# Batch 0's softmax of A by row exps on ScalarE, and a new order of work, in a fused attention and feed-forward kernel

## The chip, the cores and the metric

The kernel runs on one core of a Trainium2 chip. The metric is the device time of one execution in microseconds (us); the profile is one execution taken by the hardware profiler. Engines are PE (TensorE matmul), PEld (its weight loads), ACT (ScalarE), DVE (VectorE), POOL (GpSimd) and SP (SyncE). Each engine works through its own list of instructions in order and waits on semaphores for the others. DMA queues are fed by POOL (all loads) and SP (all stores but the last).

## The reference

Eight batches and eight heads of 576 tokens and 64 columns go through an attention with 32 landmarks (mean of 18 tokens each), and its output, as 4608 rows of 512, through a feed-forward layer of width 2048 with a squared relu. Inputs and output are f32.

```python
q_lm = q.reshape(B, H, m, S // m, D).mean(axis=3)        # m = 32, S = 576, D = 64
k_lm = k.reshape(B, H, m, S // m, D).mean(axis=3)
def sm(a, b):
    s = scale * np.matmul(a, b.transpose(0, 1, 3, 2))
    s = s - np.max(s, axis=-1, keepdims=True)
    e = np.exp(s)
    return e / (np.sum(e, axis=-1, keepdims=True) + 1e-09)
A, Bm, C = sm(q, k_lm), sm(q_lm, k_lm), sm(q_lm, k)
Z = Bm.transpose(0, 1, 3, 2) / (norm1(Bm) * norminf(Bm) + 1e-06)
for _ in range(6):
    Z = 2 * Z - Z @ Bm @ Z
x = (A @ Z @ C @ v).transpose(0, 2, 1, 3).reshape(4608, 512)
h = np.maximum(x @ w_in, 0.0)
out = (h * h) @ w_out
```

## The kernel before

The kernel never forms x. Per batch it makes Z·C·V, multiplies that by w_in (four chunks, W, whose copies to bf16, We, are the weights WP) and then multiplies A's transpose (AT) by it: F, the first feed-forward layer. R is the relu of an F (PSUM to the buffers RS, of which there are three), Q its square (RS to G), and O the second layer, by tiles of 128 tokens in four quarters of four matmuls each, with Oe as copy out of PSUM and St as store.

An operation has a name such as F0.16: kind, batch, number. Those that the text uses are, beside F, R, Q, O, W, We: SC and SA, the score matmuls for C and A; Amx, Asb, Aex, Asu, Arc, Aml, the maximum, subtraction, exp, sum, reciprocal and product of A's softmax (L959 to L971); Ap and Ab, A's transposition on PE and its copy to AT; Cmx, Cex and CT, C's maximum, exp with a running sum, and transposition; CV, C·V and CVe, its copy; N and U, matmuls and update of one Newton step; Yi and Zi, its start; Zd and Zm, the last Z spread and scaled; ZC and ZCe, Z·C·V and its copy; Bsb, Bex and so on, the same softmax for Bm; Btr, Bnm, Bad, Brn, Blo, its transposition and norms; bk, the product BK from which SA of batches 0 and 1 is made; lm, lmc, lme, landmarks, with LS as buffer; c0 to c18, constants; ldq, ldk (buffers X), ldv (V), lx (XS), win and wout, loads.

Batches 0 and 1 have A with tokens on the partitions: 18 row groups of 32 columns for each of the two head halves, 36 in all, in two parts (u = 0: 16 groups, u = 1: 20). In batch 0 each part is cut in two pieces a and b, so Asb0.1a and Aex0.1a work on 10 groups (128x320), Asb0.0a and Aex0.0a on 8 (128x256). For batch 0 the F's come in two parts of tokens too: F0.0 to F0.14 with 256 tokens, F0.16 to F0.30 with 320, a pair of ff-blocks each; the same for batch 1.

A text table, ORDER, lists every operation of the kernel in one sequence, with the PSUM banks after @ and, where there is a choice, the engine after a slash (A: ACT, D: DVE, P: POOL). A class Plan walks through it with a cost for each operation and puts dummy matmuls (a block of ones, L1177) into PE's gaps up to the first O0, which keep the granted clock up; the instructions are then emitted by the starts that this plan gives. So the table alone sets what stands where on each engine, and the plan's constants set only how the engines' lists are interleaved and where dummies go.

The lines of batch 0's A that the change touches, before:

```python
op(f"Amx{b}.{u}{z}", {"DVE": v_(w)}, ... nc.vector.tensor_reduce(s3(0)[:, at], p3_(pS)[:, at], axis=AX.X, op=ALU.max), ...)
op(f"Asb{b}.{u}{z}", {"DVE": v_(w)}, ... nc.vector.tensor_tensor(sa3[:, at], p3_(pS)[:, at], b3(0)[:, at], ALU.subtract), ...)
op(f"Aex{b}.{u}{z}", {"ACT": a_(w)}, ... nc.scalar.activation(sa3[:, at], sa3[:, at], AF.Exp), ...)
```

Of the kernel before, what the change touches and what calls it, by code (L numbers as in the profile page):

```python
# [7 lines left out]
P = 128  # L8
# [7 lines left out]
B = 8  # L16
# [18 lines left out]
N_RS = 3  # L35
# [19 lines left out]
class Plan:  # L55
# [44 lines left out]
    def schedule(self, order):  # L100
# [5 lines left out]
        for word in order:  # L106
# [5 lines left out]
            t = max([free[e], *(d.end + self.LAT[d.kind][i] for d in o.deps)])  # L112
# [17 lines left out]
            if e == "PE":  # L130
                free[e] += self.SWITCH * (o.mode != mode)
# [72 lines left out]
RATE = {"sw": 0.375e6, "hw": 0.2e6, "first": 0.385e6, "then": 0.4e6, "late": 0.3e6}  # L204
# [5 lines left out]
def a_(n):  # L210
    return 0.1 + 0.00084 * n
# [48 lines left out]
def pe(n, k=1):  # L260
    return k * max(n * 0.0004215, 0.027)
# [3 lines left out]
def kernel(  # L265
# [31 lines left out]
    LS = [mk(f"LS{i}", [P, 2, 256], F32) for i in range(2)]  # L297
# [55 lines left out]
    op("c3", {"DVE": 0.3}, lambda e: nc.vector.tensor_copy(ident[:], identf[:]),  # L353
# [991 lines left out]
```

## Time and profile before

| | |
|---|---|
| median of 3 runs | 263.11 us (262.78 to 264.88) |
| profiled execution | 263.91 us, its span 261.9 us |
| mean granted clock of PE | 0.999 |
| PE busy | 250.5 us, 96% of the span |
| DVE busy | 212.9 us, 81% |
| ACT busy | 176.3 us, 67% |
| POOL busy | 72.3 us, 28% |
| first F starts | 28.96 us |
| batch 1's first F starts | 53.74 us |
| last matmul ends | about 257.7 us |
| size of one load: X, w_in, w_out | 288, 256, 512 KB |

How to read the rows. In a timeline a row begins with start and duration in us; the brackets at its end give the idle time of the engine ahead of it and what released it. In a list of groups a row has line, engine, operation, names and shapes (partitions x elements), count, then busy us and mean ns of one, then idle time ahead and its releasers. A window row gives the window, its length, and the busy time of each engine with the count of instructions. Names in rows are those of buffers: ST is the Newton state, SA the scores of A, smA their maxima and sums, ps a PSUM bank, RS and G the relu's and the square's output, ZM the scaled Z, C the exps of C. Line numbers are those of the kernel before unless a row is from the kernel after.

### The profile page before, as it was taken

How to read it: one execution, taken by the hardware profiler on the slowest of the kernel's cores; microseconds unless marked ns; L12 is line 12 of the kernel's file. 1: busy time of each engine (PE TensorE's matmuls, PEld its weight loads, DVE VectorE, ACT ScalarE, POOL GpSimd, SP SyncE). 2: the span in 40 equal slices, each digit the busy share in tenths (PEclk: the TensorE clock that was granted, in tenths of full speed). 3: DMA queues.
4: the chain of work that ended last, by engine and by line, in shares of the span. 5: the costliest groups of instructions: out<-in, count | busy, mean ns of one | idle time of the engine just before them, and what ended most of it. 6: DMA issues, size and time to landing. Idle time of an engine off the chain costs nothing.

```text
span 261.9 us, 7574 instructions
## 1 busy us (share of the span) xinstructions
PE 250.5 (96%) x3098; PEld 140.4 (54%) x3098; DVE 212.9 (81%) x552; ACT 176.3 (67%) x325; POOL 72.3 (28%) x121
## 2 busy tenths in 40 slices
PE   7978998999999999999999999999999999999993
PEld 2565565566454556465554555565444556466542
DVE  3989799987899998978999899988999979746220
ACT  2533795859696889887765699796584674676412
POOL 8558878543500622352030210012100111000000
PEclk9999999999999999999999999999999999999999
DMA  6999999999997699999928193030302030051025
GB/s 99 206 198 201 208 206 207 207 212 224 241 218 156 100 213 222 231 169 237 208 38 165 17 201 90 0 83 1 83 17 68 21 83 20 3 121 40 3 68 132
DMA packets 25122, 34.17 MB, mean 130 GB/s; under 512 B 2432, under 2 KB 14464, under 8 KB 25088
## 3 DMA queue, kind: packets, MB, share of 16 engines
q0 software_dynamic: 19168, 24.25, 54.4%
q1 hardware_dynamic: 5760, 9.31, 13.9%
q8 instruction: 24, 0.39, 0.6%
q10 hardware_dynamic: 160, 0.13, 0.2%
q14 instruction: 10, 0.08, 0.1%
HBM read 48.50 MB, written 9.44 MB: 221 GB/s over the span
## 4 chain that ended last, share of the span: by engine, by line
PE 65%; DVE 20%; ACT 3%; issue 3%; POOL 1%; DVEq 0%; ACTq 0%; POOLq 0%
PE ps L1103 37%; PE ps L1056 17%; PE ps L892 3%; DVE G L1086 2%; ACT RS L1077 2%; DVE SA L1016 1%; DVE TT L470 1%; PE ps L735 1%; DVE smA L1020 1%; DVE sm L773 1%; DVE SA L1009 1%; PE ps L1177 1%; PE ps L821 1%; DVE RS L1079 1%; DVE smA L1012 1%
## 5 line engine op out<-in xcount | busy, mean ns | idle before, releaser
L1103 PE MATMUL ps<-w_out,G 128*128 128x512 bf16 (+1 forms) x592 | 139.4, 374 | 0.2 <-DVE LM L418 0.2
L1103 PEld LDWEIGHTS <-G 128*128 128x128 bf16 x592 | 54.4, 98 | 53.7 <-issue 6.2
L1077 ACT ACTIVATE RS<-ps 128x576 bf16<-128x576 f32 (+2 forms) x101 | 63.8, 656 | 23.8 <-PE ps L1056 15.4
L1056 PE MATMUL ps<-AT,WP 128*128 128x288 bf16 (+2 forms) x512 | 75.0, 286 | 1.1 <-DVE LM L531 1.1
L1056 PEld LDWEIGHTS <-WP 128*128 128x128 bf16 x512 | 48.0, 98 | 22.7 <-issue 2.5
L1084 ACT ACTIVATE G<-RS 128x576 bf16<-128x576 bf16 (+2 forms) x60 | 40.2, 685 | 1.8 <-DVE RS L1079 1.0
L1086 DVE TENSOR_TENSOR G<-RS 128x576 bf16<-128x576 bf16 (+2 forms) x63 | 29.3, 473 | 5.8 <-ACT RS L1077 5.3
L412 ACT COPY OS<-ps 128x512 f32<-128x512 f32 (+1 forms) x29 | 16.6, 571 | 19.0 <-PE ps L1103 15.2
L1079 DVE TENSOR_SCALAR RS<-ps 128x576 bf16<-128x576 f32 (+1 forms) x27 | 19.8, 735 | 10.0 <-PE ps L1056 8.8
L412 ACT CAST WP<-ps 128x1024 bf16<-128x1024 f32 (+1 forms) x24 | 22.4, 964 | 5.3 <-PE ps L892 5.2
L470 DVE STREAM_TRANSPOSE TT<-X 128x576 uint32<-128x576 uint32 x32 | 24.3, 762 | 0.4 <-DMA X<-in_q_dram 0.3
L636 POOL TENSOR_TENSOR BD<-ST,blkb 128x256 bf16<-128x256 bf16 x13 | 9.9, 758 | 49.3 <-DVE ST L713 42.2
L441 POOL DMA_DIRECT2D V<-in_v_dram x24 | 12.9, 539 | 25.2 <-PE ps L821 19.3
L776 ACT ACTIVATE C<-ps,sm 128x576 bf16<-128x576 f32 x16 | 14.2, 904 | 7.1 <-DVE sm L773 7.0
L713 DVE SCALAR_TENSOR_TENSOR ST<-ST,ps 128x128 bf16<-128x128 bf16 (+1 forms) x48 | 12.8, 267 | 6.0 <-PE ps L699 3.2
L1177 PE MATMUL ps<-onesb 128*128 128x512 bf16 (+1 forms) x43 | 12.4, 392 | 1.5 <-DVE onesb L348 1.5
L416 DVE CAST WP<-ps 128x1024 bf16<-128x1024 f32 (+1 forms) x10 | 11.6, 1161 | 1.6 <-PE ps L892 1.6
L773 DVE TENSOR_REDUCE sm<-ps 128x1 f32<-128x576 f32 x16 | 11.7, 744 | 0.2 <-PE ps L735 0.2
L1018 ACT ACTIVATE SA<-SA 128x640 f32<-128x640 f32 (+1 forms) x12 | 8.1, 685 | 4.8 <-DVE SA L1016 4.8
L892 PE MATMUL ps<-w_in,ZC 64*32 64x512 bf16 x256 | 10.7, 382 | 0.5 <-DVE ST L713 0.4
L657 POOL TENSOR_TENSOR ST<-Bf,sm 128x64 bf16<-128x64 f32 x5 | 1.5, 296 | 34.8 <-DVE sm L630 34.8
L1009 DVE STREAM_TRANSPOSE SA<-ps 128x320 f32<-128x320 f32 (+1 forms) x24 | 10.0, 453 | 0.9 <-PE ps L730 0.8
(140 smaller groups left out, 297.2 us busy)
## 6 DMA issues: line engine op xcount, KB each, us to landing
out_dram<-OS SPq DMA_DIRECT2D x70, 128.0 KB, 2.4
X<-in_k_dram POOLq DMA_DIRECT2D x16, 288.0 KB, 9.9
X<-in_q_dram POOLq DMA_DIRECT2D x16, 288.0 KB, 9.2
XS<-in_q_dram POOLq DMA_DIRECT2D x5, 576.0 KB, 11.6
XS<-in_k_dram POOLq DMA_DIRECT2D x5, 576.0 KB, 8.1
V<-in_v_dram POOLq DMA_DIRECT2D x8, 288.0 KB, 9.6
w_in<-in_moe_w_in_dram POOLq DMA_DIRECT2D x8, 256.0 KB, 9.4
w_out<-in_moe_w_out_dram POOLq DMA_DIRECT2D x4, 512.0 KB, 10.9
```

The source lines that it names most:

```text
L412: nc.scalar.copy(o, i)
L470: op(f"T{b}.{t}{r}", {"DVE": v_(576)}, lambda e, r=r: nc.vector.transpose(tt[:, t, r].rearrange("p s m e -> p (s m e)").bitcast(U32), x[:, ...
L773: op(f"Cmx{b}.{r}", {"DVE": v_(576)}, lambda e, r=r: nc.vector.tensor_reduce(s_[:, 12 + r:13 + r], cbanks(r), axis=AX.XY, op=ALU.max, nega ...
L776: op(f"Cex{b}.{r}", {"ACT": a_(576) + 0.27}, lambda e, r=r: nc.scalar.activation(Cs[r][:].rearrange("p x u -> p u x"), cbanks(r), AF.Exp, ...
L892: nc.tensor.matmul(ps[quad(pos_a(c, r)), pW.at + r, :], lhsT=zcs[r][half, pos_c(c, r), :], rhs=w_in[half, c, 512 * ch:512 * ch + 512], sta ...
L1056: nc.tensor.matmul(ps[:, ph.at + i, 0:w], lhsT=wp[:, r, 128 * ff:128 * ff + 128], rhs=at[:, r, t0:t0 + w], start=(r == 0), stop=(r == 1))
L1077: nc.scalar.activation(rs, pair(ph, w), AF.Relu)
L1079: nc.vector.tensor_scalar(out=rs, in0=pair(ph, w), scalar1=0.0, scalar2=None, op0=ALU.max)
L1084: nc.scalar.activation(g, rs, AF.Square)
L1086: eng(e).tensor_tensor(g, rs, rs, ALU.mult)
L1103: nc.tensor.matmul(bank(po)[:, 0:c1 - c0], lhsT=G[:, f, lo:lo + P], rhs=w_out[:, f, c0:c1], start=(f == 0), stop=(f == NF - 1))
L1177: nc.tensor.matmul(ps[:, j, 0:w], lhsT=onesb[:, 0:P], rhs=x[:, 0:w], start=True, stop=True)
```

## The change

Batch 0's four pieces of A leave out the subtraction. Their maximum is written with its sign turned (`negate`), and the exp is taken straight from PSUM, one activation for each of the 36 row groups, 128x32, with the group's column of the negated maximum as bias. The relu buffers RS go from three to four, the landmark buffer LS from two to one. Some constants may be made by ACT. Many of the plan's costs are set anew. ORDER is replaced as a whole; of its assignments 25 squares move to ACT and 36 to DVE, five on POOL become two, 27 relus on DVE become 22, and Zi0, bk1, Blo1 and Aml0.0a go from POOL to DVE. `B_ROW` is empty, so its branch for Bm is not used.

The first place is DVE, between the first update of batch 0's Newton iteration and the transposition of batch 1's inputs; L713 is that update (U0.0 and on), L962 the subtraction, L966 the sum. Before:

```order
L713 SCALAR_TENSOR_TENSOR ST_1_98<-ST_0_97,ps 128x128
L962 TENSOR_TENSOR SA_77<-ps,smA_120 128x320
L959 TENSOR_REDUCE smA_121<-ps 128x8
L962 TENSOR_TENSOR SA_77<-ps,smA_120 128x320
L713 SCALAR_TENSOR_TENSOR ST_0_97<-ST_1_98,ps 128x128
L962 TENSOR_TENSOR SA_78<-ps,smA_121 128x256 x2
L966 TENSOR_REDUCE smA_120<-SA_77 128x10
L713 SCALAR_TENSOR_TENSOR ST_1_98<-ST_0_97,ps 128x128
```

The same place after; L726 is the update, L987 the sum, L973 the maximum, L811 and L813 the scaling of C:

```order
L726 SCALAR_TENSOR_TENSOR ST_1_97<-ST_0_96,ps 128x128
L987 TENSOR_REDUCE smA_119<-SA_76 128x10
L811 RECIPROCAL sm_117<-sm_117 128x2
L990 RECIPROCAL smA_119<-smA_119 128x10
L813 TENSOR_TENSOR CMX_113<-cmk,sm_117 128x16
L726 SCALAR_TENSOR_TENSOR ST_0_96<-ST_1_97,ps 128x128
L973 TENSOR_REDUCE smA_120<-ps 128x8
L987 TENSOR_REDUCE smA_119<-SA_76 128x10
L726 SCALAR_TENSOR_TENSOR ST_1_97<-ST_0_96,ps 128x128
L973 TENSOR_REDUCE smA_120<-ps 128x8
```

The four subtractions are gone; sums and maxima stand in their place, and the maximum of the second 128x256 piece, which stood ahead of the first update, now stands behind it.

The second place is POOL, where loads are issued, around w_out. L425 loads X of batch 2, L441 V of batch 1, L456 w_out, L971 is Aml, L1086 a square. Before:

```order
L425 DMA X_64<-in_q_dram 128x1152
L425 DMA X_64<-in_k_dram 128x1152
L425 DMA X_64<-in_q_dram 128x1152
L441 DMA V_66<-in_v_dram 32x1152
L1086 TENSOR_TENSOR G<-RS_126 128x2x256
L441 DMA V_66<-in_v_dram 128x1152
L456 DMA w_out<-in_moe_w_out_dram 128x4x512 x2
L971 TENSOR_TENSOR An_79<-SA_77,smA_120 128x640
L456 DMA w_out<-in_moe_w_out_dram 128x4x512 x2
```

The same place after, where L449 loads w_in, L992 is Aml and L670 is Zi1:

```order
L449 DMA w_in<-in_moe_w_in_dram 64x4x512 x3
L992 TENSOR_TENSOR An_78<-SA_76,smA_119 128x320
L456 DMA w_out<-in_moe_w_out_dram 128x4x512 x2
L425 DMA X_64<-in_k_dram 128x1152
L992 TENSOR_TENSOR An_79<-SA_77,smA_120 128x256
L456 DMA w_out<-in_moe_w_out_dram 128x4x512
L425 DMA X_64<-in_q_dram 128x1152
L670 TENSOR_TENSOR ST_0_98<-Bf_105,sm_118 128x2x32
L425 DMA X_64<-in_q_dram 128x1152
```

The first two quarters of w_out now stand right behind w_in, and the loads of batch 2's X and batch 1's V that stood ahead of them stand behind or between.

The third place is ACT, in batch 0's feed-forward part; L1077 is a relu, L776 an exp of batch 1's C, L964 an exp of A. Before:

```order
L964 ACTIVATE SA_77<-SA_77 128x640
L412 CAST AT_81<-ps 128x640
L1077 ACTIVATE RS_127<-ps 128x512
L776 ACTIVATE C_84,sm_119<-ps,sm_119 128x2x288
L776 ACTIVATE C_85,sm_119<-ps,sm_119 128x2x288
L1077 ACTIVATE RS_125<-ps 128x512
L1077 ACTIVATE RS_126<-ps 128x640
```

After, where L1098 is a relu, L1105 a square and L789 the exp of C:

```order
L1098 ACTIVATE RS_127<-ps 128x512
L1105 ACTIVATE G<-RS_127 128x2x256
L1098 ACTIVATE RS_127<-ps 128x640
L1105 ACTIVATE G<-RS_126 128x2x320
L789 ACTIVATE C_83,sm_118<-ps,sm_118 128x2x288
L789 ACTIVATE C_84,sm_118<-ps,sm_118 128x2x288
L414 ACTIVATE LS<-ps 64x256 x2
```

The exps of batch 1's C stood behind the fourth of batch 0's relus; now the last two relus that ACT makes for batch 0, and two squares, stand right ahead of them. On PE likewise N1.3 and SC1.0 stood among the first F0; now all F0 and O1.0, O3.0, O1.1, O1.2, O3.1 stand ahead of them, and between them and F1.2 ten more quarters.

The diff, cut to its core (of the table two lines of each):

```diff
-N_RS = 3
+N_RS = 4
...
-    BLOCK, FETCH, FETCH_LOADED, PROLOG, STALL = 256, 3.8, 6.2, 94, 0.1
-
-    SWITCH = 0.092
+    BLOCK, FETCH, FETCH_LOADED, PROLOG, STALL = 256, 3.8, 6.2, 94, 0.0
+
+    SWITCH = 0.094
...
-RATE = {"sw": 0.375e6, "hw": 0.2e6, "first": 0.385e6, "then": 0.4e6, "late": 0.3e6}
+RATE = {"sw": 0.375e6, "hw": 0.2e6, "first": 0.385e6, "then": 0.4e6, "late": 0.385e6}
...
-    LS = [mk(f"LS{i}", [P, 2, 256], F32) for i in range(2)]
+    LS = mk("LS", [P, 2, 256], F32)
...
-    op("c6", {"DVE": 0.2}, c_blk, R=["msel"], W=["blkb"])
+    op("c6", {"DVE": 0.2, "ACT": 0.22}, c_blk, R=["msel"], W=["blkb"])
...
-                op(f"Amx{b}.{u}{z}", {"DVE": v_(w)}, lambda e, s3=s3, p3_=p3_, pS=pS, at=at:
-                   nc.vector.tensor_reduce(s3(0)[:, at], p3_(pS)[:, at], axis=AX.X, op=ALU.max),
+                by_row = (b, u, z) in BY_ROW
+                op(f"Amx{b}.{u}{z}", {"DVE": v_(w)}, lambda e, s3=s3, p3_=p3_, pS=pS, at=at, neg=by_row:
+                   nc.vector.tensor_reduce(s3(0)[:, at], p3_(pS)[:, at], axis=AX.X, op=ALU.max, negate=neg),
                    R=[pS], W=kx_("amx"))
...
+                def rows(e, s3=s3, sa3=sa3, p3_=p3_, pS=pS, x0=x0, x1=x1):
+                    for x in range(x0, x1):
+                        nc.scalar.activation(sa3[:, x], p3_(pS)[:, x], AF.Exp, bias=s3(0)[:, x:x + 1])
+                if by_row:
+                    op(f"Aex{b}.{u}{z}", {"ACT": ROW * (x1 - x0)}, rows, R=[pS, *kx_("amx")], W=kx_("sa"))
+                else:
+                    op(f"Asb{b}.{u}{z}", {"DVE": v_(w)}, lambda e, sa3=sa3, p3_=p3_, pS=pS, b3=b3, at=at:
+                       nc.vector.tensor_tensor(sa3[:, at], p3_(pS)[:, at], b3(0)[:, at], ALU.subtract),
+                       R=[pS, *kx_("amx")], W=kx_("sa"))
+                    op(f"Aex{b}.{u}{z}", {"ACT": a_(w)}, lambda e, sa3=sa3, at=at: nc.scalar.activation(
+                        sa3[:, at], sa3[:, at], AF.Exp), R=kx_("sa"), W=kx_("sa"))
...
+BY_ROW = ((0, 0, "a"), (0, 0, "b"), (0, 1, "a"), (0, 1, "b"))
+B_ROW = ()
+ROW = 0.12
...
-N1.1@2 F0.2@4 ldk2.0 U1.1 T1.10 F0.0@0 ldq2.0 R0.2 N1.2@6 ldv1.11 R0.0 SC1.0@4,2 U1.2 Q0.2/P
-Q0.0/A N1.3@1 Ap0.1@6 Aex1.1 U1.3 Cmx1.0 ldv1.00 F0.4@0 Ab0.1/A wout0 Asu1.1 R0.4 SA1.0@7 wout1
+We0.00 U1.0 F0.4@6 Amx1.0 We0.2 ldv1.11 N1.1@3 T1.11 F0.2@1 R0.4 U1.1 F0.0@4 Asb1.0 R0.2 ldk2.1
+N1.2@3 R0.0 W0.3@6 U1.2 F0.6@0 Q0.4 We0.3 Q0.2 F0.18@2 F0.20@4 R0.6 R0.18/D F0.16@6 wout3 R0.20
```

274 lines of the change are left out of this document (140 added, 134 removed).

## The prediction

> **What bounds the kernel now.** I read the page's totals first, then a table of windows cut where the first matmul of the feed-forward part (F) starts, where batch 1's first one starts and where the last matmul ends, and only then single waits.
>
> ```profile
> span 261.9 us, 7574 instructions
> PE 250.5 (96%) x3098; PEld 140.4 (54%) x3098; DVE 212.9 (81%) x552; ACT 176.3 (67%) x325; POOL 72.3 (28%) x121
> ```
> ```profile
> 0.00:28.96 28.96, 24.37 (x406) 14.12 (x407) 22.17 (x73) 11.34 (x33) 20.32 (x41) 1.00 1.03 180
> 28.96:53.74 24.78, 23.31 (x370) 14.65 (x367) 22.43 (x54) 20.03 (x37) 18.38 (x26) 1.00 1.20 206
> 53.74:257.70 203.96, 202.68 (x2327) 111.66 (x2325) 168.28 (x427) 144.60 (x256) 33.63 (x56) 1.00 0.59 115
> 257.70:261.90 4.20, 0.14 (x2) 0.00 (x0) 0.00 (x0) 0.37 (x1) 0.00 (x0) 0.91 0.46 113
> ```
> The columns are the window and its length, then busy time of PE, PE's weight loads, DVE, ACT and POOL, the granted clock, DMA share and GB/s. From 53.74 on PE is busy 202.68 of 203.96 us: what is left there (1.28 us) is the most that any order can win. The chain of waits says the same: late in the run it is whole blocks of second-layer matmuls back to back, four quarters in 3.45 us, 0.86 us each.
>
> ```profile
> 244.37 3.45 PE ps L1103 x16
> ```
> So the change can win only ahead of 53.74. There PE is not short of work altogether, it is short of work that is ready. In 28.96 to 53.74 it was idle 1.47 us, and 0.57 us of its busy time were dummies (L1177); second-layer matmuls (L1103) made seven quarters, 28 matmuls:
>
> ```profile
> 28.96:53.74 24.78, 6.84 (x28) 2.44 (x28) 1.00 1.20 206
> 28.96:53.74 24.78, 0.57 (x2) 0.19 (x2) 1.00 1.20 206
> ```
> The idle time stands at a few places (timeline; in brackets the idle time before a row):
>
> ```profile
> 25.89 0.30 PE L865 MATMUL ps<-ZM,CV 128*64 128x32 bf16 x7 [0.74 <-issue]
> ...
> 32.76 0.63 PE L941 MATMUL ps<-BK,TT 128*128 128x128 bf16 x8 [0.34 <-ACT AT L412]
> ...
> 40.30 1.86 DVE L1086 TENSOR_TENSOR G<-RS 128x512 bf16<-128x512 bf16 x1
> ...
> 40.60 1.26 POOL L1086 TENSOR_TENSOR G<-RS 128x640 bf16<-128x640 bf16 x1
> ...
> 42.55 1.03 PE L1056 MATMUL ps<-AT,WP 128*128 128x256 bf16 x8 [1.05 <-DVE LM L531]
> ```
> The largest, 1.05 us ahead of 42.55, is a bank that waits for a DVE held up by one square of 1.86 us that ran beside POOL's. Idle plus dummies, 1.47 + 0.57 = 2.04 us, is what a dense stretch could take out here; ZC0's 0.74 lies ahead of it.
>
> **The change part by part.** Rows for the place where the scores of batch 0 (A) become probabilities:
>
> ```profile
> 15.19 0.18 ACT L776 ACTIVATION_READ_ACCUMULATOR C<-ps,sm 128x1 f32 x1
> ...
> 17.09 0.29 DVE L713 SCALAR_TENSOR_TENSOR ST<-ST,ps 128x128 bf16<-128x128 bf16 x1 [0.34 <-POOL ST L657]
> ...
> 17.29 0.48 DVE L962 TENSOR_TENSOR SA<-ps,smA 128x320 f32<-128x320 f32 x1
> ...
> 17.70 0.41 DVE L959 TENSOR_REDUCE smA<-ps 128x8 f32<-128x256 f32 x1
> ...
> 24.37 0.38 DVE L847 TENSOR_TENSOR ZM<-ps,CRS 128x256 bf16<-128x256 f32 x1
> ...
> 27.37 0.62 PE L892 MATMUL ps<-w_in,ZC 64*32 64x512 bf16 x16
> ...
> 28.96 1.03 PE L1056 MATMUL ps<-AT,WP 128*128 128x256 bf16 x8
> ...
> 53.74 0.49 PE L1056 MATMUL ps<-AT,WP 128*128 128x256 bf16 x3
> ```
> ```profile
> L962 DVE TENSOR_TENSOR SA<-ps,smA 128x320 f32<-128x320 f32 x2 | 1.0, 482 | 0.0
> L966 DVE TENSOR_REDUCE smA<-SA 128x10 f32<-128x320 f32 x2 | 0.9, 470 | 0.0
> ...
> L959 DVE TENSOR_REDUCE smA<-ps 128x8 f32<-128x256 f32 x2 | 0.8, 416 | 0.0
> L959 DVE TENSOR_REDUCE smA<-ps 128x20 f32<-128x640 f32 x1 | 0.8, 825 | 0.1
> L962 DVE TENSOR_TENSOR SA<-ps,smA 128x640 f32<-128x640 f32 x1 | 0.8, 817 | 0.0
> L962 DVE TENSOR_TENSOR SA<-ps,smA 128x256 f32<-128x256 f32 x2 | 0.8, 417 | 0.0
> ...
> L627 DVE TENSOR_SCALAR sm<-sm 128x2 f32<-128x2 f32 x1 | 0.4, 395 | 0.0
> ...
> L1086 DVE TENSOR_TENSOR G<-RS 128x640 bf16<-128x640 bf16 x5 | 2.4, 477 | 0.3 <-ACT RS L1077 0.3
> ```
> DVE up to Zm0. DVE starts an operation about 0.08 us before the one ahead ends (17.29 + 0.48 against 17.70), so each costs its mean less 0.08. Between U0.0 (17.09) and Zm0 (24.37) the four subtracts go: 2 x 0.40 + 2 x 0.34 = 1.48 us. By the order, there now also stand one more sum (0.39), one more max (0.34), and, taken over from POOL, ACT or from behind Zm0: Aml0.0a and CVe0.1 (256 columns, 0.34 each), BK's product bk1 (512 bf16 columns, which I take as 0.34 too, since L1086 does 640 such columns in 0.477), and the small Blo1, c8 and a reciprocal (0.14 each: 65 ns per 64 columns by the two L962 rows leave 0.22 for 64 columns). That is 2.17; Btr1 (0.14) goes behind Zm0. Net +0.55. The subtracts are thus no gain at this place: DVE is filled up again.
>
> ACT, where four exps become 36. Before shows no exp of 128x32 from PSUM with a pointer bias. The nearest rows:
>
> ```profile
> L1077 ACT ACTIVATE RS<-ps 128x512 bf16<-128x512 f32 x11 | 6.4, 604 | 2.9 <-PE ps L1056 2.1 <-PE ps L842 0.7
> L1084 ACT ACTIVATE G<-RS 128x576 bf16<-128x576 bf16 x44 | 29.5, 681 | 1.7 <-DVE RS L1079 1.0
> ...
> L412 ACT CAST WP<-ps 128x1024 bf16<-128x1024 f32 x21 | 20.9, 1018 | 3.3 <-PE ps L892 3.3
> ...
> L414 ACT ACTIVATE C<-C,sm 128x576 bf16<-128x576 bf16 x2 | 1.6, 799 | 0.0
> ...
> L570 ACT ACTIVATE Bl<-Bl 128x64 f32<-128x64 f32 x8 | 2.0, 254 | 1.8 <-DVE Bl L568 1.7
> ...
> L412 ACT COPY cmk<-msel 128x4 f32<-128x4 f32 x2 | 0.3, 192 | 3.1 <-POOL msel L360 3.1
> ```
> The two 128x4 copies are 192 ns each but 0.3 us together, so the second added about 0.10 us; 32 columns instead of 4 add some 0.02. That makes 0.12, the lower end, if the pointer is free. It isn't at 576 columns: with a pointer 799 ns (L414), without 681 (L1084), 118 ns more. The upper end has no overlap at all: Bex's 254 ns, less 27 for half its columns, plus 118, makes 0.345. Half of the pointer's price overlapping leaves 0.18, which I take, being nearest to the row of back-to-back small copies. So ACT works 36 x 0.18 = 6.5 us (4.3 to 12.4), from the end of C's exps (15.19 + 0.18) to about 22, where it stood idle for much of the time: 11.34 of 28.96 us busy. ACT's gap hides the work but not its end: the last sum waits for the last row, about 0.5 us on DVE.
>
> By the Trainium skill, "ScalarE: Activation LUTs", section "What ACT_TABLE_LOAD costs", an activation with a pointer bias takes about 280 ns + 0.833 ns a column, 93 ns of which overlap the next: 0.214 us a row by that rule as an estimate, 7.7 us in all, and 1.2 us of the gain gone. L414 against L1084 agrees that a pointer costs (118 ns here, 93 there).
>
> From Zm0 to the first F. Zm0 starts at 24.37 + 0.55 + 0.5 less some 0.3 of DVE's old idle time: 25.1. Then DVE carries Zm0 0.30, Amx1.1 0.75, Btr1 and Bnm1 0.28, Bad1 0.32, Asb1.1 0.82 (27.57); ACT then Aex1.1, some 0.6 (the exp of 640 columns lies beside its neighbours), and We0.1, a cast of 1024 columns, 1.02 less 0.1. F0.4 starts at about 29.1, 0.15 us later than 28.96.
>
> What PE has done by then. Ap0.1, SA1.0 and W0.2 have moved ahead of it. Their rows:
>
> ```profile
> 31.20 0.41 PE L982 MATMUL ps<-ident,An 128*128 128x128 bf16 x2
> ...
> 31.81 0.60 PE L1056 MATMUL ps<-AT,WP 128*128 128x256 bf16 x4
> ```
> Ap0.1 took 31.20 to 31.81, 0.61; SA1.0, from 32.76, 0.56; W0.2 half of the 0.55 in which two chunks ran at 27.37, 0.28. N1.1 (0.2) is now behind. 1.25 us of work has thus gone into time that PE sat waiting before.
>
> The stretch behind it. Batch 1's attention (N1.3, SC1.0 and on) now stands behind all 16 F0 and five second-layer quarters, and 15 quarters instead of 7 stand ahead of F1.2: while a relu or a square is late there is a quarter to run. The idle and dummy time of 28.96 to 53.74 goes, 2.04 us. One new wait remains: the F0.16 group needs We0.3 on an ACT with 20.03 busy of 24.78 us before and now more relus at once, 0.25 us. F1.2 itself starts at 53.74 + 8 x 0.86 for the quarters, less 0.28 for W1.2, which now follows it, and less the gain: about 57.5. The w_out loads move ahead of X2 and V1: one of 512 KB takes some 2.5 us at 206 GB/s, an X of 288 KB 1.4; four X and three V now follow, so w_out comes 8 to 9 us sooner and X2 that much later. The nearest need, by the same rate, has 1.4 us to spare (O1.2): no cost; without that cover each late load costs its lateness on PE.
>
> The remaining edits (fourth relu buffer, one LS buffer, constants copied by ACT, plan costs) I set at nothing: they lie in ACT's idle time of the first 15 us, or only feed the order.
>
> Sum: -0.15 + 1.25 + 2.04 - 0.25 = 2.9 us gained. The profiled execution took 263.9; 263.9 - 2.9 = 261.0. It lay 0.8 above the median of 263.1, so the forecast is 260.2.
>
> **The rivals.** DVE takes it back. Once PE stands earlier, DVE must be too; it has little room in these windows:
>
> ```profile
> 66.00:85.40 19.40, 19.40 (x289) 9.41 (x288) 18.27 (x53) 14.03 (x26) 2.87 (x6) 1.00 1.02 200
> 85.40:104.40 19.00, 18.90 (x273) 11.09 (x271) 18.16 (x52) 16.74 (x31) 7.20 (x13) 1.00 1.02 178
> ```
> Its slack is 1.13 + 0.84 = 1.97 us, less than the 2.9 to be kept. If DVE ends last there, 0.9 goes, or, with both windows' slack half lost, 1.9: a gain of 1 to 2, at 262.1 to 261.1. Against it: four subtracts and five relus less on DVE.
>
> Rows cost 0.21 to 0.24 us: the pointer's 0.118 does not overlap at all (0.12 + 0.118 = 0.24), or for three quarters (0.21). 36 x 0.03 to 0.06 = 1.1 to 2.2 us later at Zm0, one for one, so 261.3 to 262.4. The rule of the Trainium skill's page on ScalarE, cited above, falls here.
>
> More. Rows at 0.12, no wait of the last sum (0.5), ZC0's 0.74 gone: 1.5 to 3 more, 257 to 258.7.
>
> Slower. The rows do not overlap: the bias column and PSUM make each start when the one ahead has ended, 0.345. Then 36 x 0.165 = 5.9 us later at the last sum, Arc, Aml, Zm0 and the first F, with nothing for PE but dummies: 263.1 + 5.9 - 2.9 = 266.1. It decides from 0.26 us a row (break-even), 0.33 for 1%. For it: no row shows exps with a pointer close together. Against: the copies of 128x4 do overlap.
>
> It does not do what it says: F0 is not dense because squares on DVE are late; the gain is then 1.25 - 0.15, 262.0, near the first rival and counted there.
>
> **How the numbers follow.** About 1% (2.6 us: below 260.5, above 265.7) is what a measurement can tell from no change. Forecast 0.45, with its own range 258.8 to 261.7; DVE 0.17; dearer rows 0.12; more 0.14; slower 0.12. Faster: six tenths of the forecast's case and all of "more", 0.41. Slower: the last case but for 0.01 between break-even and 1%, 0.11. The rest, 0.48, is within 1%. The range, 257.0 to 265.0, leaves out the top of "slower" and the tail of "more".
>
> **What would show it.** A row exp near 0.18 us start to start; Zm0 near 25.1 and the first F near 29.1; no dummies and under 0.5 us of idle PE from there to F1.2 near 57.5 with 15 quarters done; w_out landing from about 32.5; F2 and F3 earlier by 2.9. It is wrong if the rows run past 23, if PE waits for relus or loads in the stretch, or if DVE ends last before F2 and F3.

## The result and the profile after

| | before | after |
|---|---|---|
| median | 263.65 us (16 runs, 262.78 to 266.61) | 261.12 us (16 runs, 260.46 to 263.27) |
| ratio, 95% interval | | 0.9904 (0.9877 to 0.9931) |
| span of the profiled execution | 261.9 us | 259.4 us |
| first F / batch 1's first F | 28.96 / 53.74 us | 30.41 / 59.13 us |

About 1% faster, 2.5 us. The lines that answer to those shown of before, from the page of the profile after:

```profile
span 259.4 us, 7586 instructions
PE 249.6 (96%) x3094; PEld 139.6 (54%) x3094; DVE 210.0 (81%) x547; ACT 181.1 (70%) x362; POOL 67.9 (26%) x117
```

The windows of the kernel after, cut at the same events (window and length, then busy PE, PEld, DVE, ACT, POOL, clock, DMA share, GB/s), and the middle one for the second layer's line (L1124) and the dummies' (L1198) alone:

```profile
0.00:30.41 30.41, 26.35 (x419) 14.42 (x419) 20.84 (x70) 18.10 (x70) 20.18 (x41) 1.00 1.05 180
30.41:59.13 28.72, 28.12 (x384) 16.32 (x377) 23.89 (x60) 22.06 (x41) 12.97 (x21) 1.00 1.19 215
59.13:255.20 196.07, 194.97 (x2301) 108.89 (x2299) 165.31 (x419) 140.62 (x252) 34.79 (x57) 1.00 0.58 113
255.20:259.40 4.20, 0.11 (x2) 0.00 (x0) 0.00 (x0) 0.37 (x1) 0.00 (x0) 0.89 0.39 94
```
```profile
30.41:59.13 28.72, 14.28 (x60) 5.49 (x60) 1.00 1.19 215
30.41:59.13 28.72, 0.00 (x0) 0.00 (x0) 1.00 1.19 215
```

The two F at its ends, in the timeline of PE:

```profile
30.41 0.61 PE L1077 MATMUL ps<-AT,WP 128*128 128x256 bf16 x4
...
59.13 0.60 PE L1077 MATMUL ps<-AT,WP 128*128 128x256 bf16 x4
```

The stretch from the first F to F1.2 is nearly as dense as it was forecast: no dummies, 60 matmuls of the second layer (15 quarters) and 0.60 us idle where before had 1.47. Of the 0.60, 0.55 is one stop that the section on e10 looks at. But the stretch begins 1.45 us later than before's, not 0.15, and F1.2 stands at 59.13, not at 57.5.

Where PE's time went is easier to see against its work than against the clock. I gave every kind of PE operation its usual start-to-start time in before and asked at what time each kernel had done the same sum of work. The lead of the kernel after over before is then:

| before's clock | kernel after is at | lead, us |
|---|---|---|
| 29.0 | SA1.0, 29.3 | -0.1 |
| 36.9 | F0.10, 35.9 | 1.0 |
| 47.5 | O0.0, 44.5 | 2.3 |
| 53.7 | O1.3, 50.9 | 2.4 |
| 59.0 | O2.2, 58.3 | 1.35 |
| 69.1 | O5.1, 67.8 | 0.7 |
| 81.2 | SS3.1, 80.8 | 0.4 |
| 94.5 | O8.2, 93.1 | 1.2 |
| 107.2 | O10.1, 106.6 | 0.6 |
| 145.0 | F4.2, 143.5 | 1.5 |
| 164.1 | CV5, 161.5 | 2.1 |
| 214 to the end | | 2.5 |

So some 2.4 us are won in the dense stretch, 2.0 of them are gone again by 81 us, and 2.1 others are won behind it. That the end agrees with the forecast hides this. The early figures hang on the price that each kind of operation is given: with the mean of its start-to-start times in before (behind 53.74 us, where it occurs there) the lead at 53.7 is 2.0; with the same mean after each time is limited to 0.1 above the kind's median it is 2.8. From 59 us on both agree with the table within 0.2.

The first F's delay, in the timeline of DVE, after (brackets: idle time ahead and its releaser); L973 is the maximum, L987 the sum, L978 the row exp, L860 Zm0:

```profile
17.39 0.49 DVE L973 TENSOR_REDUCE smA<-ps 128x10 f32<-128x320 f32 x1 [0.89 <-ACT SA L978]
...
17.99 0.48 DVE L987 TENSOR_REDUCE smA<-SA 128x10 f32<-128x320 f32 x1
...
19.84 0.49 DVE L987 TENSOR_REDUCE smA<-SA 128x10 f32<-128x320 f32 x1 [0.55 <-ACT SA L978]
...
21.26 0.42 DVE L973 TENSOR_REDUCE smA<-ps 128x8 f32<-128x256 f32 x1 [0.74 <-ACT SA L978]
...
26.32 0.42 DVE L860 TENSOR_TENSOR ZM<-ps,CRS 128x256 bf16<-128x256 f32 x1
```

And ACT's side of it, the timeline and the group of the 36 row exps:

```profile
15.48 1.88 ACT L978 ACTIVATE SA<-ps,smA 128x32 f32<-128x32 f32 x10
17.92 3.31 ACT L978 ACTIVATE SA<-ps,smA 128x32 f32<-128x32 f32 x18 [0.56 <-DVE smA L973]
```
```profile
L978 ACT ACTIVATE SA<-ps,smA 128x32 f32<-128x32 f32 x36 | 6.7, 326 | 0.8 <-DVE smA L973 0.8
```

The second maximum (17.39) needs nothing of the first piece's exps; it starts 0.03 us after they end (15.48 + 1.88 = 17.36). The 640 scores of this part lie in two PSUM banks of 512 columns, so the second piece shares the first bank, which ACT is reading until then. At 21.26 it is the same, with both pieces in one bank. The other thing that the two engines share is the buffer smA, whose maxima ACT reads as bias. It isn't the cause: the sum at 17.99 writes other columns of the same smA while ACT's next rows read it (17.92 to 21.23), and does not wait. By the Trainium skill, "PSUM — Partial Sum Buffer", section "PSUM bank collisions raise a hardware error", two engines must be kept apart by bank and quadrant of partitions, reads against reads too; the program has a wait of DVE on ACT there (0.89 and 0.74 us), which agrees; no run here leaves it out. Before, the subtraction and the maximum were both on DVE and no such wait arose.

### The profile page after: what moved, and what is told of

Its sections match the earlier page's. It is cut to its first block, busy times and chain, and to the rows that moved or that the text cites. A ratio compares the mean times of both kernels' runs of the same rounds, so it can differ in the third digit from the quotient of the medians.

```text
span 259.4 us, 7586 instructions
## 1 busy us (share of the span) xinstructions
PE 249.6 (96%) x3094; PEld 139.6 (54%) x3094; DVE 210.0 (81%) x547; ACT 181.1 (70%) x362; POOL 67.9 (26%) x117
## 4 chain that ended last, share of the span: by engine, by line
PE 73%; DMA 12%; POOL 5%; issue 4%; ACT 3%; DVE 1%; POOLq 0%
PE ps L1124 42%; PE ps L1077 19%; DMA XS<-in_k_dram 9%; DMA X<-in_q_dram 3%; PE ps L905 3%; ACT SA L978 2%; PE ps L834 2%; POOL X L425 1%; PE ps L486 1%; PE ps L748 1%; POOL V L441 1%; PE ps L1003 1%; POOL BD L649 1%; PE ps L1198 1%; PE ps L712 1%
## 5 line engine op out<-in xcount | busy, mean ns | idle before, releaser
L1124 PE MATMUL ps<-w_out,G 128*128 128x512 bf16 (+1 forms) x592 | 138.0, 374 | 0.0
L1124 PEld LDWEIGHTS <-G 128*128 128x128 bf16 x592 | 54.2, 98 | 54.4 <-issue 5.7
L1098 ACT ACTIVATE RS<-ps 128x576 bf16<-128x576 f32 (+2 forms) x106 | 64.9, 652 | 14.2 <-PE ps L1077 7.0
L1077 PE MATMUL ps<-AT,WP 128*128 128x288 bf16 (+2 forms) x512 | 72.2, 286 | 0.1
L1077 PEld LDWEIGHTS <-WP 128*128 128x128 bf16 x512 | 47.9, 98 | 20.0 <-issue 2.9
L1105 ACT ACTIVATE G<-RS 128x576 bf16<-128x576 bf16 (+2 forms) x50 | 33.5, 687 | 1.7 <-DVE RS L1100 1.2
L1107 DVE TENSOR_TENSOR G<-RS 128x576 bf16<-128x576 bf16 (+2 forms) x76 | 32.4, 447 | 2.2 <-ACT RS L1098 1.6
L412 ACT COPY OS<-ps 128x512 f32<-128x512 f32 (+1 forms) x31 | 17.7, 572 | 21.7 <-PE ps L1124 20.9
L412 ACT CAST WP<-ps 128x1024 bf16<-128x1024 f32 (+1 forms) x23 | 21.6, 981 | 3.9 <-PE ps L905 3.7
L789 ACT ACTIVATE C<-ps,sm 128x576 bf16<-128x576 f32 x16 | 14.2, 904 | 10.7 <-DVE sm L786 10.6
L441 POOL DMA_DIRECT2D V<-in_v_dram x24 | 12.8, 534 | 30.6 <-PE ps L834 22.8
L1100 DVE TENSOR_SCALAR RS<-ps 128x576 bf16<-128x576 f32 (+2 forms) x22 | 16.4, 752 | 4.5 <-PE ps L1077 3.8
L726 DVE SCALAR_TENSOR_TENSOR ST<-ST,ps 128x128 bf16<-128x128 bf16 (+1 forms) x48 | 12.6, 263 | 5.2 <-PE ps L712 2.0
L1198 PE MATMUL ps<-onesb 128*128 128x512 bf16 (+1 forms) x41 | 12.5, 413 | 1.6 <-DVE onesb L348 1.6
L416 DVE COPY OS<-ps 128x512 f32<-128x512 f32 x6 | 4.1, 688 | 10.1 <-PE ps L1124 10.0
L905 PE MATMUL ps<-w_in,ZC 64*32 64x512 bf16 x256 | 10.2, 382 | 0.0
L425 POOL DMA_DIRECT2D X<-in_k_dram x16 | 9.3, 582 | 2.5 <-DMA w_out<-in_moe_w_out_dram 1.0
```

The costliest lines, as they stand in the source:

```text
L412: nc.scalar.copy(o, i)
L416: eng(e).tensor_copy(o, i)
L441: lambda e, r=r, p0=p0, n=n, src=src: nc.gpsimd.dma_start(vv[32 * p0:32 * (p0 + n), r].rearrange("p s d -> p (s d)"), src),
L905: nc.tensor.matmul(ps[quad(pos_a(c, r)), pW.at + r, :], lhsT=zcs[r][half, pos_c(c, r), :], rhs=w_in[half, c, 512 * ch:512 * ch + 512], sta ...
L1077: nc.tensor.matmul(ps[:, ph.at + i, 0:w], lhsT=wp[:, r, 128 * ff:128 * ff + 128], rhs=at[:, r, t0:t0 + w], start=(r == 0), stop=(r == 1))
L1098: nc.scalar.activation(rs, pair(ph, w), AF.Relu)
```

## The experiments

All compare with runs of before on the same chip (medians 263.8 to 263.9; 263.65 for after). The chip is not the same for all, so versions are best compared by their ratios. Spans are those of the profiled executions: 261.9 before, 259.4 after.

| | median | ratio to before (95%) | span | first F |
|---|---|---|---|---|
| after | 261.12 | 0.9904 (0.9877 to 0.9931) | 259.4 | 30.41 |
| e1 Zm0 four times | 262.84 | 0.9948 (0.9922 to 0.9973) | 260.9 | 31.79 |
| e2 maxima first | 261.06 | 0.9895 (0.9838 to 0.9951) | 259.0 | 30.36 |
| e3 subtractions back | 260.45 | 0.9850 (0.9807 to 0.9893) | 258.7 | 30.42 |
| e4 buffers alone | 263.27 | 0.9965 (0.9935 to 0.9995) | 261.6 | |
| e5 after to 75 us, then before | 263.93 | 1.0009 (0.9987 to 1.0031) | 262.0 | |
| e6 before to 75 us, then after | 262.95 | 0.9961 (0.9934 to 0.9988) | 261.6 | |
| e7 after to 141 us, then before | 263.12 | 0.9962 (0.9936 to 0.9988) | 261.5 | |
| e8 before to 141 us, then after | 263.10 | 0.9968 (0.9950 to 0.9987) | 261.4 | |
| e9 e2 without five dummies | 260.85 | 0.9883 (0.9852 to 0.9913) | 259.7 | 30.14 |
| e10 after, 12 dummies split | 261.40 | 0.9908 (0.9876 to 0.9940) | 258.9 | 30.79 |
| e11 row exps in before's order | 265.94 | 1.0068 (1.0033 to 1.0102) | 262.6 | |
| e12 e3 with loads moved | 260.72 | 0.9863 (0.9830 to 0.9896) | 258.8 | |

### e1: a delay ahead of the first F

> The changed kernel with the product Zm0 done four times instead of once, 3 x 0.34 = 1.0 us more on DVE right ahead of ZC0. Theory (what is won or lost ahead of the first F passes to the end one for one, because PE is full behind it): Zm0's end, the first F and the end all 1.0 later, 262.1 against 261.1. Rival (DVE or later waits swallow it between 50 and 105 us): the end 0 to 0.4 later, 261.1 to 261.5.

```diff
-            op(f"Zm{b}", {"DVE": v_(256)}, lambda e: nc.vector.tensor_tensor(
+            op(f"Zm{b}", {"DVE": v_(256)}, lambda e: [nc.vector.tensor_tensor(
...
-                crs[:].unsqueeze(3).to_broadcast([P, 4, 2, M]), ALU.mult),
+                crs[:].unsqueeze(3).to_broadcast([P, 4, 2, M]), ALU.mult) for _ in range(1 if b else 4)],
```

Timeline of e1, DVE and PE:

```profile
26.35 1.79 DVE L860 TENSOR_TENSOR ZM<-ps,CRS 128x256 bf16<-128x256 f32 x4
...
28.20 0.30 PE L878 MATMUL ps<-ZM,CV 128*64 128x32 bf16 x8 [1.20 <-DVE ZM L860]
...
31.79 0.61 PE L1077 MATMUL ps<-AT,WP 128*128 128x256 bf16 x4
```

Three more products took 1.79 - 0.42 = 1.37 us, more than the 1.0 expected. The first F is 1.38 later, the span 1.5, the median 1.7. Here a loss ahead of the first F reached the end in full, although in after most of the lead is gone by 81 us.

### e2 and e9: the wait for the shared bank taken away

> The changed kernel with the maximum of the second piece of each part moved ahead of the first piece's row exps, so that DVE need not wait for ACT to be done with the same PSUM bank (0.89 and 0.74 us in the trace). Theory (passed on one for one): Zm0 and the first F 0.6 to 0.8 earlier and the end too, 260.4. Rival (swallowed later): Zm0 as much earlier, the end within 0.2 of 261.1. Second rival (the Newton chain or the loads set Zm0 anyway): Zm0 itself moves by less than 0.2.

In the order, `Amx0.1b` now stands right behind `Amx0.1a`, and `Amx0.0b` behind `Amx0.0a`, ahead of the row exps that read the same bank. Timeline of e2, DVE and PE:

```profile
25.14 0.42 DVE L860 TENSOR_TENSOR ZM<-ps,CRS 128x256 bf16<-128x256 f32 x1
...
26.67 0.30 PE L878 MATMUL ps<-ZM,CV 128*64 128x32 bf16 x8
26.91 1.15 PE L1198 MATMUL ps<-onesb 128*128 128x512 bf16 x5
27.98 0.22 PE L663 MATMUL ps<-Bt 32*32 32x32 bf16 x8
28.13 0.66 PE L1003 MATMUL ps<-ident,An 128*128 128x128 bf16 x4
28.73 0.62 PE L905 MATMUL ps<-w_in,ZC 64*32 64x512 bf16 x16
```

Zm0 comes at 25.14, 1.18 earlier and where the prediction had it (25.1). The first F does not move: PE works off five dummies behind ZC0 and W0.1 starts at 28.73, as in after (28.77). What one engine wins is taken by what the order put next on another, here work that computes nothing.

> As e2 (the maxima ahead of the row exps), but without the five dummies of PE that stood between ZC0 and W0.1 at 26.9 to 28.1; five early dummies of 512 columns are split in two, so that the count of instructions stays. In e2 Zm0 came 1.18 us sooner and the first F not at all. Theory (the dummies, put there by a plan that takes Zm0's wait for granted, held W0.1 back; what is won ahead of the first F passes to the end): F0.4 0.6 to 0.9 sooner, 29.5 to 29.8, and the end as much, 260.3 against e2's 261.06. Rival (the gain is swallowed behind the first F): F0.4 as said, the end within 0.2 of e2. Second rival (We0.1 or a w_in load sets F0.4): F0.4 within 0.2 of 30.4.

```diff
-            nc.tensor.matmul(ps[:, j, 0:w], lhsT=onesb[:, 0:P], rhs=x[:, 0:w], start=True, stop=True)
+            for _ in range(1 + (w == 512 and len(more) < 5)):
+                v = 256 if w == 512 and len(more) < 5 else w
+                nc.tensor.matmul(ps[:, j, 0:v], lhsT=onesb[:, 0:P], rhs=x[:, 0:v], start=True, stop=True)
+            more.append(w)
...
-            o.emit(o.eng)
+            if o.name != "fill24.76":
+                o.emit(o.eng)
```

W0.1 then started at 27.41, 1.3 sooner, but the granted clock of PE fell to half in this execution (windows; the clock is the third figure from the end):

```profile
24.00:25.00 1.00, 1.00 (x10) 0.48 (x10) 1.00 (x7) 0.27 (x2) 1.00 (x2) 1.00 1.23 202
25.00:26.00 1.00, 0.79 (x8) 0.59 (x7) 1.00 (x3) 0.10 (x1) 1.00 (x3) 0.67 1.26 203
26.00:28.00 2.00, 1.86 (x37) 1.06 (x36) 1.83 (x8) 1.33 (x3) 1.96 (x4) 0.50 1.24 204
```

The first F came at 30.14, 0.2 sooner than in e2 and not the 0.6 to 0.9 of the theory. The clock fell at 25, ahead of the place of the dropped dummies (26.9), so their absence there is not shown to be the cause. It is not one odd execution: five of e9's six runs have a mean clock of 0.987, the profiled one among them, against two at 0.983 and four at 0.996 to 0.999 in e2. The median ratio, 0.9883 against 0.9895, can't be told from e2's. The one run of e9 with a mean clock of 0.999 had a span of 258.2 us, e2's four at 0.996 to 0.999 had 258.7 to 259.5: that is the way a gain that reaches the end would look, but one run doesn't show it, and whether the 1.18 us would reach the end stays open.

### e3, e4 and e11: the parts of the change

> The changed kernel's order with batch 0's four subtractions put back on DVE and the four long exps on ACT, so the row exps are gone and all else stays. Theory of the prediction (the subtractions are no gain at this place): the end within 0.5 of 261.1; DVE has 1.48 more work, but its waits for ACT's rows (0.89, 0.55, 0.74) go. Rival (the row exps carry the gain): Zm0 about 1.5 later and the end 262.5 or more.

```diff
-BY_ROW = ((0, 0, "a"), (0, 0, "b"), (0, 1, "a"), (0, 1, "b"))
+BY_ROW = ()
```

with `Asb0.1a Aex0.1a` behind CT0.0, and the other three pairs behind U0.0, `Amx0.0a` and `Amx0.0b`. The first F stands at 30.42 as with the row exps; Zm0 comes at 25.80, 0.52 sooner than in after. The span is 0.7 shorter. So the row exps, at the place that they have, bring nothing; they pay for it by the waits above. At e2's place they have Zm0 at 25.14, 0.66 sooner than the subtractions, but there the dummies take it. The 0.7 at the end is not theirs either: at CV1 of batch 1 e3 is 0.05 us ahead of after (51.88 against 51.93, rows in the section on e10), at F1.2 it is 0.67 ahead, in e3's timeline:

```profile
58.46 0.60 PE L1077 MATMUL ps<-AT,WP 128*128 128x256 bf16 x4
```

Between the two lies the stop that e10 is about.

> The kernel before with its own order word for word and its subtractions, and of the change only the four relu buffers (taken in the order of the table, not by number), the one LS buffer and the plan's new costs, which move dummies alone. Theory (the buffers are worth nothing by themselves, as the order was made for three): 263.1 to 263.9, within 0.4 of before. Rival (a relu waits for a buffer somewhere in before, and its late waits at 86 to 164 us come from that): 261.5 to 262.5.

```diff
-N_RS = 3
+N_RS = 4
...
-            i = rs_n[0] % N_RS
-            rs_n[0] += 1
+            i, key = RS_AT[f"R{b}.{f + NF * u}"], ("RS", b, f + NF * u)
```

0.35% faster, by an interval that ends just below one (0.9995), 0.3 in the span. The trace says more than this total. Three of its rows of PE:

```profile
29.54 1.03 PE L1077 MATMUL ps<-AT,WP 128*128 128x256 bf16 x8
...
105.55 1.02 PE L1123 MATMUL ps<-w_out,G 128*128 128x512 bf16 x3
...
163.87 0.29 PE L881 MATMUL ps<-ZM,CV 128*128 128x64 bf16 x4
```

The first F is 0.57 us late (29.54 against 28.96), with other dummies ahead of it, and yet the end is 0.3 early. The order is before's, so the two can be compared F by F: e4 is 0.6 behind up to 102 us, gains 0.30 between 102 and 106, 0.34 between 160 and 164 and 0.30 between 211 and 216, and ends 0.35 ahead. Before's waits at 105.27 and 163.95 (their rows stand in the section on e5 to e8) are gone, the second but for 0.13. So behind the first F the old order wins 0.95 us with four buffers that are taken as they come free. A PE that comes late could also find more work ready. That is not what took the wait at 163.95 away, since e11 below is another 1.1 us later and has the same 0.14 left of it, and being late can't bring the end ahead of before's. The change takes its four buffers by number, so the 0.95 can't be carried over to it as it is.

> The order of before with its four subtractions dropped and the row exps in the place of the four exps, buffers as in e4: the change's first part without the new order. To be read against e4 (263.27). Theory (no gain at this place: DVE's 1.48 us go, but ACT's 5 us more, and DVE and ACT wait for each other at the shared banks): 263.0 to 264.5. Rival (the row exps carry the gain and the order only uses it): 262.3 or less.

The edit is e4's with `BY_ROW` as in the change and the four Asb dropped from the order. 265.94 against e4's 263.27, more than the 263.0 to 264.5 that the theory expected; the rival, that the row exps carry the gain, falls. By itself the change's first part costs 1.0 us in the span and more in the runs. The first F stands at 30.64, 1.10 behind e4's, and behind it e11 wins 1.0 at the three places where e4 does. DVE's timeline in e11 shows the cost:

```profile
19.77 0.49 DVE L987 TENSOR_REDUCE smA<-SA 128x10 f32<-128x320 f32 x1 [1.01 <-ACT SA L978]
...
22.89 0.74 DVE L987 TENSOR_REDUCE smA<-SA 128x8 f32<-128x256 f32 x2 [1.11 <-ACT SA L978]
```

DVE's sums wait for rows that take longer than the subtractions they replace.

### e10: a wait that belongs to a place in the instruction stream

In after, PE stops inside CV1, a run of very short matmuls, behind the 69th of 72 recorded, for nothing that the trace shows:

```profile
51.93 0.80 PE L834 MATMUL ps<-V,CT 32*64 32x128 bf16 x69
53.28 0.25 PE L834 MATMUL ps<-V,CT 32*64 32x128 bf16 x3 [0.55 <-issue]
```

In e3, whose plan puts 13 dummies more ahead of it, it doesn't (one row of e3's timeline):

```profile
51.88 0.97 PE L834 MATMUL ps<-V,CT 32*64 32x128 bf16 x72
```

> The changed kernel with 12 of its first dummies of 512 columns split into two of 256: the same work, 12 matmuls (24 instructions with their weight loads) more ahead of CV1, as the version with the subtractions has 13 more. Theory (CV1's 0.55 us of waiting for nothing that the trace shows, after its 69th matmul, hangs on where in the instruction stream CV1 lies): the wait is gone, the end 0.5 to 0.7 sooner, 260.5, like the version with the subtractions. Rival (that version is faster because of its exps): the wait stays or goes, the end within 0.2 of 261.1.

```diff
-        for w in [512] * (n // 2) + [256] * (n % 2):
-            nc.tensor.matmul(ps[:, j, 0:w], lhsT=onesb[:, 0:P], rhs=x[:, 0:w], start=True, stop=True)
+        for w in [512] * (n // 2) + [256] * (n % 2):
+            for _ in range(1 + (w == 512 and len(more) < 13)):
+                v = 256 if w == 512 and len(more) < 13 else w
+                nc.tensor.matmul(ps[:, j, 0:v], lhsT=onesb[:, 0:P], rhs=x[:, 0:v], start=True, stop=True)
+            more.append(w)
```

Timeline of e10, PE:

```profile
25.60 0.31 PE L957 MATMUL ps<-BK,TT 128*64 128x128 bf16 x3 [0.36 <-issue]
...
52.26 0.89 PE L834 MATMUL ps<-V,CT 32*64 32x128 bf16 x72
```

CV1 runs through, and PE stops for 0.36 us inside SA1.1 instead, which delays the first F by 0.38. The span is 0.5 shorter, the median (261.40) isn't: the total is not settled by these runs. Four of the six have a mean clock of 0.990; the two at 1.000 have spans of 258.9 and 259.2, those of after at 0.998 and more 258.7 to 259.8. But that the same work stops at another place when 24 instructions are put ahead of it is shown, and it repeats: in all six traces with after's number of dummies ahead of CV1 (after, e1, e2, e5, e7, e9) PE stops behind the 69th matmul, for 0.18 to 0.62 us, though CV1 starts anywhere from 51.82 to 53.33; in the three with 12 or 13 matmuls more (e3, e10, e12) it never does. So the stop goes with the place in the stream and not with the time. Here is e1's, whose CV1 starts 1.4 us later:

```profile
54.75 0.25 PE L834 MATMUL ps<-V,CT 32*64 32x128 bf16 x3 [0.62 <-issue]
```

What the stop is, the traces do not say. The 0.74 in front of 25.89 that the prediction lists for before has the same mark, "issue". e3's lead over after is at this place: between O1.3 and O2.0 after loses 0.9 us, e3 0.25.

### e5 to e8: one order's head with the other's tail

> The order of the kernel after up to F1.26 (about 75 us), and from there on the order of before; the rest of the change (row exps, buffers) as after. In the traces the work done by PE at this place is 0.4 us ahead of before. Theory A (the parts add up, and most of the gain arises behind 75 us by the new order's fewer waits there): 0.4 to 0.9 faster than before. Theory B (the gain of the first 45 us, 2.4, is what reaches the end; where it seems lost at 75 PE has merely done other work first): 2 or more faster.

> The order of before, with its subtractions, up to F1.26 (about 75 us), and from there on the order of the kernel after; buffers as after. Theory A (parts add up): the late part alone brings about 2.1 over before. Theory B (the gain is the head's): within 0.6 of before, which the buffers alone gave.

> The order of the kernel after up to F4.0 (about 141 us), and from there on that of before; row exps and buffers as after. In the traces PE is 1.3 to 1.5 us ahead at this place. Theory A (parts add up): 1.3 to 1.5 faster than before. Theory B (the gain is the head's and all of it is there early): 2.5. Theory C (before's waits at 140 and 164 us go by themselves once the head is ahead): 2 or more as well, and those waits are gone from the trace.

> The order of before, with its subtractions, up to F4.0 (about 141 us), and from there on that of the kernel after; buffers as after. Theory A (parts add up): 1.0 to 1.2 faster than before, with no wait of PE over 0.3 us from 141 on. Theory B (the gain is the head's): within 0.6 of before.

The edit in each is the order's table: up to the named F from one kernel, then all that is left, in the other's sequence. For e5 and e6 the F named is F1.26, for e7 and e8 it is F4.0; relu buffers are taken as in e4 in all four.

No half brings the whole. Where the two halves meet, PE waits for what the other order would have had ready; the largest such waits, timelines of e6 and of e7:

```profile
80.54 0.29 PE L748 MATMUL ps<-TT,LT 32*32 32x288 bf16 x1 [1.19 <-ACT RS L1097]
```
```profile
143.78 2.12 PE L1077 MATMUL ps<-AT,WP 128*128 128x288 bf16 x16 [1.33 <-DVE OS L416]
```

Read behind the seam, by the same account of work done, the new tail wins: in e6 from -1.6 at 81 us to +0.35 at the end (2.0; in after 2.1), in e8 from -0.55 at 145 us to +0.46 (1.0; in after 1.0). The old tail behind the new head wins nothing in e5 from 81 us to the end (-0.15 to -0.1). But from 145 us on the old tail wins too, 0.6 in e5 (-0.7 to -0.1) and 0.6 in e7 (-0.3 to +0.4), as much as e4 and e11 win there with before's order. All four halves have e4's buffers. So of the 1.0 that the new tail wins behind 145 us, 0.6 can be had with the old order and these buffers, and no run separates what the new order does from what they do. A part of the 2.0 of e6 may also be what any order regains behind a stop such as the one at its seam.

The totals missed theory A's sums, which had no price for the seam: by the medians e5 was to gain 0.4 to 0.9 and gained nothing, e6 2.1 and gained 0.9, e7 1.3 to 1.5 and gained 0.7, e8 1.0 to 1.2 and gained 0.7. The last three can't be told from the 0.6 of e4, the buffers alone. Theory B, that all of the gain is the head's, wanted 2 or more in e5 and falls there, though e5 also loses 0.46 us in a stop marked "issue" at 109.33. What before's tail waits for, in the timeline of before:

```profile
105.27 1.02 PE L1103 MATMUL ps<-w_out,G 128*128 128x512 bf16 x4 [0.21 <-DVE LM L418]
...
140.50 0.41 PE L892 MATMUL ps<-w_in,ZC 64*32 64x512 bf16 x8 [0.40 <-DVE ST L713]
...
163.95 0.29 PE L868 MATMUL ps<-ZM,CV 128*128 128x64 bf16 x4 [0.48 <-ACT G L1084]
```

After has none of these three. e4, with before's order, still has the second (0.39 at 140.76) and neither of the others, so those two go without the new order, with e4's buffers. e5 has the second too (0.40 at 141.22), but is 0.7 behind before there, so this says nothing on theory C; that falls by e7, which was to gain 2 or more.

### e12: a late wait taken out

After and e3 have one wait that before has not, 0.73 and 0.71 us at 103 us for XS, the input of batch 5's landmarks.

> The version with the subtractions (e3) with four loads that are needed only after 130 us (two of batch 5's V, one each of batch 6's X and batch 4's V, issued at 84 to 86 us) moved behind the loads of batch 5's landmark inputs XS, for which PE waits 0.71 us at 102.5. Theory (XS lands late only because those four stand ahead of it in POOL's queue; what PE gains there reaches the end): the wait goes, the end 0.5 to 0.7 below e3's 260.45, about 259.8. Rival (DVE or the squares set that place next): the wait goes, and another within 5 us takes most of it, the end within 0.2 of e3. Second rival: one of the four now lands too late and PE waits for it around 134 or 160 us.

In the order `ldv5.11 ldv5.00 ldk6.0 ldv4.00` now stand behind `lx5.0 lx5.1 ldq5.1 ldq7.1`. The wait is gone and e12 leads e3 by 0.6 at O10.1; 4 us later the lead is lost. e12's timeline there:

```profile
106.41 0.96 PE L905 MATMUL ps<-w_in,ZC 64*32 64x512 bf16 x16
107.30 1.90 PE L1124 MATMUL ps<-w_out,G 128*128 128x512 bf16 x7
109.47 0.20 PE L659 MATMUL ps<-Bt,BD 128*128 128x32 bf16 x2 [0.27 <-ACT WP L412]
```

The chunks W3 (L905) took 0.63 in e3 and now 0.96, and behind them stands a wait for ACT's copy of them. The first rival was right in the trace: ACT and DVE, not PE, set that place, and 260.72 (0.9863) is no better than 260.45 (0.9850). Of the versions here e3 has the lowest median, and by its interval it is faster than before; against after (0.9807 to 0.9893 beside 0.9877 to 0.9931) the intervals overlap.

## Why the prediction was right, and where it was not

The time (260.2 forecast, 261.1 measured) and the sign were right. More than half of what the time is off lies in its base, the median of three runs (263.11) where 16 have 263.65; in differences it is 2.9 against 2.5. The dense stretch came too, by five, then ten more quarters in front of F1.2 and without dummies. That what is won in it is what the end shows did not hold: e5 has the new head and the old tail, and gains nothing. Of its terms:

- *A row costs 0.18 us.* Right: 10 rows took 1.88, all 36 6.7 (6.5 forecast). Start to start it is (1.88 - 0.326) / 9 = 0.173; so 0.153 of the 0.326 overlap. By the Trainium skill, "ScalarE: Activation LUTs", section "What ACT_TABLE_LOAD costs", it would be 0.214 as an estimate, with 0.093 of overlap; the trace shows more overlap. The rivals with rows at 0.21 and more, and at 0.345, fall. That half of the pointer's price overlaps was a choice in the middle of a wide range, and no row shows that share by itself.
- *The subtractions are no gain at this place.* Right for the place that the change gives the row exps: e3.
- *Zm0 at 25.1, the first F 0.15 us later.* This step failed. It allowed one wait of 0.5 for ACT; there were three, 2.18 us in all, two of them for a PSUM bank that ACT was reading. Zm0 came at 26.32, the first F at 30.41, and the rows ended at 23.25 (21.72 + 1.53), past the 23 that the prediction names as a sign of being wrong. From Zm0 to the first F it took 4.09, as reckoned (4.0), but two paths end together there, the exp of batch 1 on ACT (at 29.43) and W0.1 on PE behind its dummies (at 29.39), and only the first was reckoned; e2, without the two bank waits, has Zm0 at 25.14 and the first F at 30.36 by the second.
- *1.25 us of work done earlier.* Right: at the first F the lead is -0.1 in spite of 1.45 us on the clock.
- *2.04 less 0.25 in the stretch.* By idle time and dummies it is 1.44 (1.47 + 0.57 against 0.60), by the lead about 2.4, 2.0 to 2.8 with the price of the kinds.
- *"What is left there (1.28 us) is the most that any order can win", behind 53.74.* This step failed twice. The lead went from 2.4 to 0.4 by 81 us: about 0.8 at CV1 (1.6 us against 0.83 in before, 0.55 of it the stop in the stream), 0.34 by a wait for a relu at SS2.1 (below), the rest in small steps of 0.1 that these traces put to no cause. And then 2.1 were won where the bound left 1.28: before's five worst places behind 81 us lose about 2.2 by start-to-start times, of which the busy share shows 1.28 as idle, all that it shows behind 53.74. A busy PE in these rows is not a PE at its pace.
- *The fourth relu buffer, "set at nothing".* This step failed. With before's own order four buffers won 0.95 us behind the first F (e4), at waits that stand in before's trace.
- *DVE takes it back* (the first rival, 0.17). Between 51 and 81 us the lead shrank by more than this rival said, but of the causes that show, the stop at CV1 and the relu on ACT, none is DVE. e12 shows that a gain of 0.6 at 103 us is taken by DVE's and ACT's work 4 us on. It did not hold to the end.
- *Loads in time.* Right for w_out: no O waits for it. At a load that the prediction didn't look at, XS, PE waits 0.73 us at 103 us; e12 takes that wait out and gains nothing at the end.
- *F2 and F3 earlier by 2.9.* Not so: F2's first matmul starts at 89.31 (before 89.27), F3's at 110.06 (before 111.31).

The wait at SS2.1 in after's timeline, and the late load:

```profile
66.46 0.27 PE L743 MATMUL ps<-TT,LT 32*32 32x256 bf16 x1 [0.34 <-ACT RS L1098]
```
```profile
103.20 0.84 PE L486 MATMUL ps<-XS,seg 96*32 96x256 bf16 x24 [0.73 <-DMA XS<-in_k_dram]
```

So the forecast of 2.9 met 2.5 by errors that nearly cancel, which is luck: 1.2 too much at the first F (a lead of 1.1 forecast, -0.1 measured), some 0.7 too little in the stretch, and 2.0 lost and 2.1 won in a part that it took for closed. What the 2.1 is made of is shown in part: e4's buffers can win 0.95 of it without the new order; how the change's buffers and its order share it is open.

## What to carry to other kernels

Before an operation is moved from DVE to ACT, look whose banks it reads: here the two engines took turns at one PSUM bank, and the turns (0.89 and 0.74 us), not the operation's price, were what the next engine waited for. Measure what an order can still win by the starts of equal work, not by the busy share of the bound engine. Test a small edit that rides along, such as one more buffer, by itself and in the trace: its gain can hide behind a loss elsewhere. And when two orders are compared, compare them at several places: a total can be right for reasons that cancel.

## What was not expected of the hardware

PE stopped for 0.55 us in the middle of CV1 and, with 24 instructions more ahead, did not stop there but for 0.36 us in SA1.1: a stop that belongs to a place in the instruction stream. Six traces have it at CV1's 69th matmul, the three with 12 or 13 matmuls more ahead do not. And in e9 PE's granted clock fell to 0.50 from 26 to 32 us, with 0.28 us of busy time in the microsecond from 22 to 23; in e2's profile, with 0.24 in that microsecond, it did not. That fall alone makes e9's mean clock 0.987, and four more of its six runs have the same mean. What sets it off is open.
